# A fused attention and gated-MLP block: three head quads share the first layer norm's stage, two tiles are transposed by TensorE, and zero products stand first

## The chip, the cores and the metric

The kernel runs on one NeuronCore of a Trainium2 chip, as one program launched once. The metric is the device time of that launch in microseconds. TensorE (PE, with its weight loads PEld), VectorE (DVE), ScalarE (ACT), GpSimd (POOL) and SyncE (SP, used here only to issue DMAs) each run their own instruction stream in order and wait for each other by semaphores.

## What is computed

One transformer block in bf16 on a sequence of 2048 rows of 1024, with 32 query heads of 32 columns that share one key head and one value head, followed by a gated MLP of width 3584:

```python
q = (x @ wq).reshape(B, S, H, Dh).transpose(0, 2, 1, 3)   # x: layernorm of A_x
k = x @ wk
v = x @ wv
scores = einsum("bhqd,bkd->bhqk", q, k) * (Dh ** -0.5)
o = einsum("bhqk,bkd->bhqd", softmax(scores), v)
h = A_x + o.transpose(0, 2, 1, 3).reshape(B, S, H * Dh) @ wo
g, u = layernorm(h) @ w_gate, layernorm(h) @ w_up
out = h + (sigmoid(g) * u) @ w_down
```

The layer norms have no learned scale. The attention is not causal.

## The kernel before

**Tiles.** The 2048 rows are 16 tiles of 128 rows (`t`) or 8 chunks of 256 (`c`, `QC`). The 32 heads are 8 *quads* of four heads (`q`): 128 columns, each head in its own 32 partitions. Keys and values are cut in 8 blocks of 256 rows (`BPG`). A *burst* is the scores of one quad, one chunk and one key block: 8 matmuls that use 32 rows of the array each (`s_burst`, L525), which fill two of the three pairs of PSUM banks in `S_ps`. ACT turns each pair into P with one exponential over 128 x 1024 elements (`one_exp`, L549): two exponentials to a burst, 512 bursts, 1024 exponentials in all. A *PV group* (L640, L643) multiplies the P of one quad and chunk with V and, for the first ten groups, with ones for the row sums; later groups get their sums from DVE additions. Everything else on PE (K, Q, V, Wo, gate, up and down) goes through two further banks, `X_ps`, one open group to a bank.

**Where P lies.** P goes into a ring of 18 half tiles, `Pr`, so nine bursts deep. A burst may start only when PV has read the tile that it overwrites (`can_s`). P of quad 0 in chunk 0 lies in `hact` instead, six half tiles deep, since it is read along the way.

**First stage.** Each tile of x is loaded by SP. DVE takes its statistics (L314, L316); POOL computes 1/sqrt(var + eps) by two powers (L325, L327) for two tiles at once. The mean is subtracted on ACT for tiles 0 to 3 (L352) and on DVE for the others (L356); DVE multiplies (L359); SP issues a DMA transpose (L419) into `xnT`. Then K of two tiles (`k_group`), Q of chunk 0 (two quads first, the others along the way) and V (`vq_group`) can be computed. K, V and Q are evicted from PSUM by ACT (L434, L465, L470). Wk is copied to four places side by side by four ACT instructions (L932), so that K comes out once for each of the four row groups.

**The loop of the first stage** has eight turns, one for each key block. A turn takes the statistics of two tiles, normalizes two others, computes one burst of quad 0, K for the next block, one burst of quad 1, V (and in the later turns one quad of Q), and a part of quad 0's PV group. 16 bursts are done when it ends.

**The rest** is a fixed order, worked out at build time by a planner that keeps a clock for each engine: it issues a burst as soon as the exponentials before it have freed the banks, and fills PE's time in between with PV groups, the remaining Q groups, Wo groups, then gate, up and down of the chunks that are ready. Wo and w_down are loaded by POOL's queue; POOL also computes the second layer norm's roots. Gate and up weights are loaded by SP, in halves of 512 KB, also into parts of QT, Pr and kT that are free by then.

Of the kernel before, what the change touches and what calls it, by code (L numbers as in the profile page):

```python
# [12 lines left out]
P = 128  # L13
DH = 32
# [69 lines left out]
def bass_sequential_preLN__grouped_kv_mqa__glu_gated_glu__prompt_kernel(  # L84
# [32 lines left out]
    G_SUM, NPB = 10, 4  # L117
    WD_AT, WD_GAP, WD_LATE = 6, 6, 6
# [5 lines left out]
    with ExitStack() as es:  # L124
# [94 lines left out]
        def _(unused):  # L219
# [98 lines left out]
            def ln_rstd(i0, n, after):  # L318
                i1 = i0 + n
                need(pool, after)  # L320
                t_ = c_pool.inc(pool.tensor_scalar(out=vz[:, i0:i1], in0=mv[:, i0:i1, 1], scalar1=EPS_B, scalar2=None,  # L321
                                                   op0=ALU.add), 0.25)
                pool.tensor_copy(out=mean[:, i0:i1], in_=mv[:, i0:i1, 0])
                need(pool, t_)
                t_ = c_pool.inc(pool.tensor_tensor(out=sd[:, i0:i1], in0=vz[:, i0:i1], in1=half[:, 0:n], op=ALU.pow), 0.9)  # L325
                need(pool, t_)
                return c_pool.inc(pool.tensor_tensor(out=rs[:, i0:i1], in0=sd[:, i0:i1], in1=none[:, 0:n], op=ALU.pow), 0.8)  # L327
# [10 lines left out]
            NSUB = 4  # L338

            def ln1_stats(t):  # L340
                st_val[t] = ln_stats(x_tile(t), t, x_val[t])
                if t < NSUB:
                    need(pool, st_val[t])
                    nm_val[t] = c_pool.inc(pool.tensor_scalar(out=nmean[:, t:t + 1], in0=mv[:, t:t + 1, 0], scalar1=-1.0,
                                                              scalar2=None, op0=ALU.mult), 0.25)
                if t % 2 == 1:
                    rs_val[t - 1] = rs_val[t] = ln_rstd(t - 1, 2, st_val[t])

            def ln1_norm(t):
                if t < NSUB:  # L350
                    need(act, nm_val[t], xnT_read.get(t - 4))
                    xc = c_act.inc(act.activation(out=xn(t), in_=x_tile(t), func=ACTF.Identity, bias=nmean[:, t:t + 1]),  # L352
                                   0.91, 0.12)
                else:
                    need(dve, rs_val[t], xnT_read.get(t - 4))
                    xc = c_dve.inc(dve.tensor_scalar(out=xn(t), in0=x_tile(t), scalar1=mean[:, t:t + 1],  # L356
                                                     scalar2=None, op0=ALU.subtract), 0.5)
                need(dve, xc, rs_val[t])
                xn_val[t] = c_dve.inc(dve.tensor_scalar(out=xn(t), in0=xn(t),  # L359
                                                        scalar1=rs[:, t:t + 1], scalar2=None, op0=ALU.mult), 0.5)  # L360
                xnT_read[t] = xnT_val[t] = transposed(sp, xnT[:, t // TPQ, :, (t % TPQ) * P:(t % TPQ + 1) * P], xn(t), t % 4, xn_val[t])
                if t == 1:
                    for i in (8, 9):
                        load_x(i)
                if t == 3:
                    for i in (10, 11):
                        load_x(i)
                    load_wq(1, 256, 256)
                if t == 5:
                    for i in (12, 13):  # L370
                        load_x(i)
                if t == 7:
                    for i in (14, 15):
                        load_x(i)
                if t in (9, 11):
                    i = (t - 5) // 2
                    load_wq(i, 256 * i, 256)
# [51 lines left out]
            def k_group(p):  # L429
                c0 = 2 * p * P  # L430

                def evac(bank, tick):
                    need(act, tick)
# [4 lines left out]
                return _Group(items, evac, [wk4_val, xnT_val[2 * p], xnT_val[2 * p + 1]])  # L438
# [11 lines left out]
            def vq_group(p, qs):  # L450

                items, after = [], [xnT_val[0], xnT_val[1]] + [wq_need(q) for q in qs]
                for i, q in enumerate(qs):
                    items += q_items(q, 0, QC, i * QC)
                if p is not None:
                    after += [wv_val, xnT_val[2 * p], xnT_val[2 * p + 1]]
# [5 lines left out]
                def evac(bank, tick):  # L462
                    need(act, tick)
                    if p is not None:
                        v = v_val[p] = c_act.inc(act.activation(  # L465
                            out=V[:, 2 * p:2 * p + 2, :], in_=bank[:, QC:QC + 2 * DH].rearrange("p (a b) -> p a b", a=2),
                            func=ACTF.Copy), 0.2, 0.1)
                    if qs:
                        n = len(qs)
                        v = c_act.inc(act.activation(  # L470
                            out=QT[:, qs[0]:qs[0] + n, 0:QC], in_=bank[:, 0:n * QC].rearrange("p (a b) -> p a b", a=n),
                            func=ACTF.Copy), 0.1 + 0.22 * n, 0.1)
                        for q in qs:
                            q_val[(0, q)] = v
# [3 lines left out]
            def q_group(q, c0, n):  # L478
                def evac(bank, tick):
                    need(dve, tick)  # L480
# [613 lines left out]
```

## Time and profile before

| | us |
|---|---|
| median of 3 runs | 1138.39 |
| lowest and highest | 1138.31, 1139.34 |
| the profiled execution, whole | 1137.37 |
| its span in the trace | 1135.6 |
| PE busy / ACT busy / DVE busy | 1085.1 / 1012.3 / 803.1 |

One execution was profiled. A row of the timeline has the start and the length in us, the engine, the line of the kernel, the operation, the tile written and the tile read, their shapes and how many instructions the row joins; in brackets stands how long the engine was idle before it and what ended that. A row of the chain of waits has only start, length, engine, tile and line. A row of stretches has the stretch, its length, and for each engine its busy time and its instructions, then the clock granted to PE (1.00 is full speed), the mean share of the DMA engines and GB/s. PE's matmuls are pipelined and their ends are modelled, so PE that is busy is not PE at its peak.

### The profile page before, as it was taken

How to read it: one execution, taken by the hardware profiler on the slowest of the kernel's cores; microseconds unless marked ns; L12 is line 12 of the kernel's file. 1: busy time of each engine (PE TensorE's matmuls, PEld its weight loads, DVE VectorE, ACT ScalarE, POOL GpSimd, SP SyncE). 2: the span in 40 equal slices, each digit the busy share in tenths (PEclk: the TensorE clock that was granted, in tenths of full speed). 3: DMA queues.
4: the chain of work that ended last, by engine and by line, in shares of the span. 5: the costliest groups of instructions: out<-in, count | busy, mean ns of one | idle time of the engine just before them, and what ended most of it. 6: DMA issues, size and time to landing. Idle time of an engine off the chain costs nothing.

```text
span 1135.6 us, 33182 instructions
## 1 busy us (share of the span) xinstructions
PE 1085.1 (96%) x14450; PEld 655.8 (58%) x14512; DVE 803.1 (71%) x1424; ACT 1012.3 (89%) x1168; POOL 58.3 (5%) x122
## 2 busy tenths in 40 slices
PE   3899999999899999999999999999999999999998
PEld 2564446764376645774477645774376645775784
DVE  7433336878978798888987789788887898884111
ACT  4899999999999999999999999999999999991110
POOL 3210001000100000000100000000100010001000
PEclk9899999999999999999999999999999999999999
DMA  9931106871256613773166613663166612769700
GB/s 230 246 125 39 39 12 176 238 214 55 39 167 192 182 29 92 199 205 86 33 182 192 181 30 102 192 194 94 34 180 189 187 39 66 205 193 249 191 1 19
DMA packets 284176, 150.90 MB, mean 133 GB/s; under 512 B 40704, under 2 KB 278272, under 8 KB 284032
## 3 DMA queue, kind: packets, MB, share of 16 engines
q1 hardware_dynamic: 276256, 138.17, 45.1%
q0 software_dynamic: 2544, 9.44, 2.5%
q10 hardware_dynamic: 5232, 1.18, 0.8%
q8 instruction: 114, 1.87, 0.7%
q14 instruction: 30, 0.25, 0.1%
HBM read 136.18 MB, written 4.19 MB: 124 GB/s over the span
## 4 chain that ended last, share of the span: by engine, by line
PE 75%; ACT 12%; DVE 8%; issue 3%; DMA 1%; POOL 1%; ACTq 0%; DVEq 0%; another core or an unknown queue 0%
PE X_ps L792 33%; PE X_ps L856 13%; PE S_ps L525 11%; ACT Pr L549 11%; PE X_ps L304 8%; PE X_ps L643 8%; DVE pairs L582 2%; DVE pairs L591 2%; PE X_ps L640 1%; DVE st L314 1%; PE X_ps L622 1%; ACT hact L549 1%; DVE hx L866 0%; DMA zone<-hn 0%; DVE st L738 0%
## 5 line engine op out<-in xcount | busy, mean ns | idle before, releaser
L549 ACT ACTIVATE Pr<-S_ps 128x1024 bf16<-128x1024 f32 x1008 | 944.7, 1127 | 1.5 <-PE S_ps L525 1.4
L582 DVE TENSOR_TENSOR pairs<-Pr 128x1024 bf16<-128x1024 bf16 x432 | 293.1, 686 | 76.1 <-ACT Pr L549 73.1
L792 PE MATMUL X_ps<-QT,wgu 128*128 128x256 bf16 x2096 | 268.7, 274 | 3.3 <-DVE hx L866 1.6
L591 DVE TENSOR_TENSOR pairs<-pairs 128x1024 bf16<-128x1024 bf16 x324 | 223.8, 691 | 21.9 <-DVE pairs L582 0.5
L792 PEld LDWEIGHTS X_ps<-QT,wgu 128*128 128x128 bf16 x2096 | 192.2, 98 | 61.9 <-issue 39.3
L856 PE MATMUL X_ps<-zone,hact 128*128 128x512 bf16 x848 | 205.4, 380 | 8.1 <-issue 4.6
L525 PE MATMUL S_ps<-QT,kT 32*128 32x256 bf16 x4096 | 204.4, 274 | 7.7 <-ACT Pr L549 4.4
L792 PE MATMUL X_ps<-QT 128*128 128x256 bf16 x1328 | 168.5, 273 | 0.0
L643 PE MATMUL X_ps<-Pr,V 128*32 128x256 bf16 x4032 | 151.2, 274 | 2.0 <-DVE hact L831 1.2
L525 PEld LDWEIGHTS S_ps<-QT,kT 32*128 32x128 bf16 x4096 | 60.8, 92 | 153.1 <-ACT Pr L549 117.0
L792 PEld LDWEIGHTS X_ps<-QT 128*128 128x128 bf16 x1328 | 123.4, 98 | 30.8 <-issue 16.9
L811 ACT ACTIVATE gu<-X_ps 128x512 f32<-128x512 f32 x112 | 73.4, 656 | 76.0 <-PE X_ps L792 75.1
L856 PEld LDWEIGHTS X_ps<-zone,hact 128*128 128x128 bf16 x896 | 78.6, 98 | 106.9 <-issue 25.5
L831 DVE SCALAR_TENSOR_TENSOR hact<-gu,X_ps 128x512 bf16<-128x512 f32 x112 | 76.6, 684 | 66.3 <-PE X_ps L792 65.0
L643 PEld LDWEIGHTS X_ps<-Pr,V 128*32 128x32 bf16 x4032 | 99.9, 96 | 24.1 <-issue 16.5
L304 PE MATMUL X_ps<-zone 128*128 128x256 bf16 (+2 forms) x512 | 79.8, 302 | 22.2 <-POOL sd L325 14.2
L661 DVE COPY ols<-X_ps 128x256 f32<-128x256 f32 x64 | 26.9, 420 | 65.3 <-PE X_ps L643 55.1
L304 PEld LDWEIGHTS X_ps<-zone 128*128 128x128 bf16 x512 | 39.5, 101 | 53.6 <-POOL sd L325 14.2
L304 PE MATMUL X_ps<-wo,QT 128*128 128x512 bf16 x242 | 59.6, 380 | 1.7 <-issue 1.6
L866 DVE SCALAR_TENSOR_TENSOR hx<-X_ps,hx 128x512 bf16<-128x512 f32 x32 | 22.0, 688 | 41.7 <-PE X_ps L856 40.8
L321 POOL TENSOR_SCALAR vz<-mv 128x1 bf16<-128x1 bf16 (+1 forms) x24 | 8.8, 365 | 828.1 <-DVE mv L742 816.4
L481 DVE CAST QT<-X_ps 128x512 bf16<-128x512 f32 (+1 forms) x32 | 20.0, 624 | 33.2 <-PE X_ps L304 33.2
(53 smaller groups left out, 430.4 us busy)
## 6 DMA issues: line engine op xcount, KB each, us to landing
wgu<-in_B_w_gate_dram SPq DMA_DIRECT2D x73, 512.0 KB, 4.7
wgu<-in_B_w_up_dram SPq DMA_DIRECT2D x58, 512.0 KB, 4.6
QT<-in_B_w_up_dram SPq DMA_DIRECT2D x49, 512.0 KB, 4.9
QT<-in_B_w_gate_dram SPq DMA_DIRECT2D x34, 512.0 KB, 4.9
zone<-in_B_w_down_dram POOLq DMA_DIRECT2D x14, 512.0 KB, 5.1
hx<-in_A_x_dram SPq DMA_DIRECT2D x16, 256.0 KB, 3.5
out_dram<-hx SPq DMA_DIRECT2D x32, 128.0 KB, 1.7
Pr<-in_B_w_up_dram SPq DMA_DIRECT2D x5, 512.0 KB, 8.3
```

Source lines behind the costliest of these rows:

```text
L304: ins = pe.matmul(sel(bank), lhsT=a, rhs=b, start=(i == 0), stop=(i == last))
L525: ins = pe.matmul(S_ps[:, bank, kt * QC:(kt + 1) * QC], lhsT=kT4[DH * j:DH * (j + 1), (2 * b + kt) * P:(2 * b + kt + 1) * P], rhs=QT[DH * ...
L549: c_e.inc(act.activation(out=p_tile(k, n % 2).rearrange("p (a b) -> p a b", a=2), in_=S_ps[:, 2 * pr:2 * pr + 2, :], func=ACTF.Exp, scale= ...
L582: add_half[k] = slot_use[slot] = c_dve.inc(dve.tensor_tensor(out=pairs[:, slot, :].rearrange("p (j q) -> p j q", j=4), in0=p4[:, :, 0, :], ...
L591: slot_use[x] = slot_use[y] = c_dve.inc(dve.tensor_tensor(out=pairs[:, x, :], in0=pairs[:, x, :], in1=pairs[:, y, :], op=ALU.add), T_ADD, ...
L643: ins = pe.matmul(bank[DH * j:DH * (j + 1), 0:QC], lhsT=V[:, 2 * b + kt, :], rhs=rhs(j), start=first and summed, stop=last and not summed, ...
L661: dve.tensor_copy(out=ols[:, 0:QC], in_=bank[:, 0:QC])
L792: ins = pe.matmul(bank[:, j * QC:(j + 1) * QC], lhsT=halves[i][:, dt, j * P:(j + 1) * P], rhs=QT[:, dt, c * QC:(c + 1) * QC], start=(dt == ...
L811: tanh_val[n] = c_act.inc(act.activation(out=slot, in_=bank, func=ACTF.Tanh, scale=0.5), T_TANH, 0.1)
L831: hact_val[(c, 2 * fp + 1)] = gu_read[n] = c_dve.inc(dve.scalar_tensor_tensor(out=hact[:, 2 * fp:2 * fp + 2, :], in0=slot.rearrange("p (a ...
L856: ins = pe.matmul(bank, lhsT=hact[:, ft, tt * P:(tt + 1) * P], rhs=wd[:, ft, dc * 512:(dc + 1) * 512], start=(ft == 0), stop=(ft == NFT - 1))
L866: v = c_dve.inc(dve.scalar_tensor_tensor(out=hv, in0=bank, scalar=0.5, in1=hv, op0=ALU.mult, op1=ALU.add), 0.61, 0.08)
```

## The change

- **Loads.** The second quarter of Wq is loaded by SP between x tiles 3 and 4 (before: after tile 11). The other x tiles and quarters follow the transposes in an order given by a table, `LOADS`.
- **Zeros.** 36 matmuls of 128 x 256 zeros stand first in PE's order, and write to `X_ps`.
- **Tiles 0 and 1** are transposed by PE: 8 matmuls each against an identity matrix into the banks of `S_ps`, evicted to `xnT` by ACT (tile 0 and half of tile 1) and DVE (the other half). The identity is built by POOL.
- **Layer norm 1** computes the root for each tile by itself. ACT subtracts the mean for tiles 0 to 2 (before: 0 to 3).
- **Wk** is copied to four places by one DVE instruction.
- **Evictions** of V and of Q from quad 1 on go to DVE; K and quad 0's Q stay on ACT.
- **Three quads.** A turn of the loop has three bursts, one of each of quads 0, 1 and 2; 24 bursts are done when it ends. P of quad 2 lies in `wo` for the first four bursts and in the second half of the columns of `QT` for the other four. Wo's load, the w_down loads behind it, and the Q groups that write those columns wait until PV has read it.
- **The ring** keeps its depth, with an offset of two half tiles (`ring_need`, `p_tile`). The exponentials and PV address P as four columns of 256 rather than two of 512.

```diff
-            for t in range(8):
+            for t in range(4):
                 load_x(t)
...
+            load_wq(1, 256, 256)
+            for t in range(4, 8):
+                load_x(t)
+            warm = pairs[:, 1, 0:256]
+            ident = pairs[:, 0, 0:P]
+            warm_val = c_dve.inc(dve.memset(warm, 0.0), 0.2)
+            c_ = c_pool.inc(pool.memset(pairs[:, 2, 0:P], 1.0), 0.4)
+            need(pool, c_)
+            ident_val = c_pool.inc(pool.affine_select(out=ident, in_=pairs[:, 2, 0:P], compare_op=ALU.is_equal, fill=0.0,
+                                                      base=0, pattern=[[-1, P]], channel_multiplier=1), 0.5)
...
+            def pe_transpose(t):
+                need(pe, xn_val[t], ident_val)
+                for dt in range(DT):
+                    ins = pe.matmul(S_ps[:, 2 * t + dt // 4, dt % 4 * P:(dt % 4 + 1) * P], lhsT=xn(t)[:, dt * P:(dt + 1) * P],
+                                    rhs=ident, start=True, stop=True)
...
+            def pe_out(eng, t, h0, h1, *ticks):
+                need(eng, *ticks)
+                dst = xnT_tile(t)[:, 4 * h0:4 * h1, :]
+                src = S_ps[:, 2 * t + h0:2 * t + h1, :].rearrange("p a (b q) -> p (a b) q", q=P)
...
                 def evac(bank, tick):
-                    need(act, tick)
-                    if p is not None:
-                        v = v_val[p] = c_act.inc(act.activation(
...
+                    if qs == [0]:
+                        need(act, tick)
+                        v = c_act.inc(act.activation(out=out, in_=src, func=ACTF.Copy), 0.33, 0.1)
+                    else:
+                        need(dve, tick)
+                        if p is not None:
+                            v = v_val[p] = c_dve.inc(dve.tensor_copy(
...
             def burst(k):
-                if k < 2 * BPG:
-                    return 0, k % 2, k // 2
+                if k < HG * BPG:
+                    return 0, k % HG, k // HG
...
+            def ring_need(k):
+                r = ring(k)
+                if r is None or r < 2 * BPG + 1:
+                    return 0
+                return r - 2 * BPG if r <= 2 * BPG + BPG else r - BPG
...
             def p_tile(k, h):
                 r = ring(k)
                 if r is None:
...
-                return Pr[:, (2 * r + h) % RP, :]
+                elif r < BPG:
+                    t = Pr[:, 2 * r + h, :]
+                elif r < BPG + 4:
+                    i = 2 * (r - BPG) + h
+                    t = wo[:, i, :]
+                elif r < 2 * BPG:
+                    c0 = (r - BPG) * QC
+                    return QT[:, 4 * h:4 * h + 4, c0:c0 + QC]
+                else:
+                    t = Pr[:, (2 * r + 2 + h) % RP, :]
+                return t.rearrange("p (a b) -> p a b", b=QC)
...
+            need(pe, warm_val)
+            for i in range(NWARM):
+                pe.matmul(X_ps[:, 1, 0:256], lhsT=warm[:, 0:P], rhs=warm, start=True, stop=True)
+            k_pe[0] = 7.0
+            ln1_stats(0)
+            ln1_stats(1)
+            need(dve, wk_val)
+            wk4_val = c_dve.inc(dve.tensor_copy(out=wk4.rearrange("p a (r j) -> p a r j", r=4),
+                                                in_=wkr.unsqueeze(2).to_broadcast([P, DT, 4, DH])), 0.6)
+            ln1_sub(0)
+            ln1_sub(1)
+            ln1_mult(0)
+            f0, f1 = pe_transpose(0)
+            xnT_val[0] = [pe_out(act, 0, 0, 2, f0, f1)]
+            ln1_stats(2, (0,))
+            ln1_mult(1)
+            f0, f1 = pe_transpose(1)
+            ln1_stats(2, (1,))
+            xnT_val[1] = [pe_out(act, 1, 0, 1, f0), pe_out(dve, 1, 1, 2, f1)]
+            ln1_sub(2)
+            ln1_stats(3)
+            ln1_mult(2)
+            ln1_out(2)
+            ln1_sub(3)
             need(pe, const_val)
             run_group(k_group(0))
-            run_group(vq_group(None, [0, 1]))
+            run_group(vq_group(None, [0]))
+            run_group(vq_group(None, [1]))
+            ln1_mult(3)
+            ln1_out(3)
+            ln1_stats(4)
             pv[0] = pv_group(0)
             for p in range(BPG):
+                k0 = HG * p
+                s_burst(k0)
+                exps(k0)
+                if p == 0:
+                    run_group(vq_group(None, [2]))
+                    ln1_stats(5)
+                else:
+                    run_group(vq_group(p, [p] if p >= HG else []))
+                s_burst(k0 + 1)
+                exps(k0 + 1)
+                if p == 0:
+                    run_group(vq_group(0, []))
+                for t in (2 * p + 4, 2 * p + 5):
+                    if t < NT:
+                        ln1_norm(t)
                 for t in (2 * p + 6, 2 * p + 7):
                     if t < NT:
                         ln1_stats(t)
...
                 if p > 0:
                     run_item(pv[0])
                     run_item(pv[0])
+                s_burst(k0 + 2)
+                if p + 1 < BPG:
+                    exps(k0 + 2, (0,))
+                    run_group(k_group(p + 1))
+                    exps(k0 + 2, (1,))
+                else:
+                    exps(k0 + 2)
...
+                if wo_val[0] is None and pv_done[0] >= 2 * BPG:
+                    need(pool, (c_pv, 2 * BPG))
+                    wo_val[0] = dma(pool, wo[:], A_wo.rearrange("(q p) n -> p q n", p=P), d_wo, 2048)
```

More of the change, by code (lines that the diff above doesn't have):

```diff
@@ L369, in ln1_norm @@
[L369 to L377, printed above, removed]
+                    xc_val[t] = c_act.inc(act.activation(out=xn(t), in_=x_tile(t), func=ACTF.Identity, bias=nmean[:, t:t + 1]),
+                                          0.91, 0.2)
+                else:
+                    need(dve, mean_val[t], xnT_read.get(t - 4))
+                    xc_val[t] = c_dve.inc(dve.tensor_scalar(out=xn(t), in0=x_tile(t), scalar1=mean[:, t:t + 1],
+                                                            scalar2=None, op0=ALU.subtract), 0.45)
@@ L427, in _, with xnT_ready, k_group @@
             k_val, v_val, q_val = {}, {}, {}
-            def k_group(p):
+            def xnT_ready(*tiles):
+                r = []
+                for t in tiles:
+                    r += xnT_val[t] if isinstance(xnT_val[t], list) else [xnT_val[t]]
+                return r
+            def k_group(p, mid=None):
                 c0 = 2 * p * P
                 def evac(bank, tick):
+                    if mid is not None:
+                        mid()
                     need(act, tick)
@@ L888, in _ @@
             pv_next = [0]
[L889 removed]
+            wd_val, wo_val = [None], [None]
             pr_given = [False]
```

181 lines of the change are left out of this document (93 added, 88 removed).

## Prediction

> **What bounds the kernel now.** I read the page first, then four stretches of the span, then the timeline of the first 60 us and the chain of waits.
>
> ```profile
> span 1135.6 us, 33182 instructions
> PE 75%; ACT 12%; DVE 8%; issue 3%; DMA 1%; POOL 1%; ACTq 0%; DVEq 0%; another core or an unknown queue 0%
> ```
>
> ```profile
> 0.00:60.00 60.00, 34.59 (x484) 22.05 (x488) 34.29 (x76) 41.91 (x62) 18.85 (x44) 0.89 1.02 244
> 60.00:140.00 80.00, 79.78 (x1359) 42.54 (x1360) 27.06 (x59) 80.00 (x90) 5.67 (x8) 1.00 0.18 57
> 140.00:1025.00 885.00, 863.26 (x11879) 519.45 (x11936) 717.48 (x1250) 881.39 (x1004) 30.91 (x62) 1.00 0.49 135
> 1025.00:1136.00 111.00, 107.48 (x746) 71.77 (x740) 24.24 (x40) 8.96 (x15) 2.87 (x8) 1.00 0.47 111
> ```
>
> The columns are PE, PEld, DVE, ACT, POOL, then the granted clock and DMA. The chain names PE, but the stretches say more. From 60 to 1025 us ACT is busy for 961 of 965 us: the exponentials run without a gap, and PE fills the time between score bursts, with 21.7 us idle in the third row. From 1025 on only PE works, on what is left. So an exponential that ends earlier pulls the whole middle forward, as far as PE can follow, and PE work left over at its end is paid in full. The first 60 us are loose: PE is idle for 25 us, ACT for 18. That is the stage changed.
>
> ```profile
> 3.78 1.29 DVE L314 BATCH_NORM_STATS2 st<-hx 128x6 f32<-128x512 bf16 x2 [3.78 <-DMA hx<-in_A_x_dram]
> 5.40 0.25 POOL L344 TENSOR_SCALAR nmean<-mv 128x1 f32<-128x1 bf16 x1 [4.49 <-DVE mv L316]
> 9.02 0.88 DVE L359 TENSOR_SCALAR zone<-zone,rs 128x1024 bf16<-128x1024 bf16 x2 [2.32 <-POOL rs L327]
> 9.54 2.72 SPq L419 DMA_TRANSPOSE zone<-zone  x2
> 14.19 4.59 PE L304 MATMUL X_ps<-zone 128*128 128x256 bf16 x24 [14.19 <-POOL sd L325]
> 18.81 0.60 ACT L470 ACTIVATE QT<-X_ps 128x512 bf16<-128x512 f32 x1 [2.34 <-PE X_ps L304]
> 19.55 0.40 PE L525 MATMUL S_ps<-QT,kT 32*128 32x256 bf16 x8 [0.78 <-ACT QT L470]
> 19.98 1.94 ACT L549 ACTIVATE hact<-S_ps 128x1024 bf16<-128x1024 f32 x2 [0.57 <-PE S_ps L525]
> 26.63 1.87 PE L304 MATMUL X_ps<-zone 128*128 128x256 bf16 x8 [3.06 <-DMA zone<-zone]
> ```
>
> The first exponential starts at 19.98: two tiles wait for the slower reciprocal root (9.02), then for transposes by DMA (9.54 to 14.19, where the releaser shown, POOL, is long done), then 24 matmuls take 4.59 us. Later K groups wait for transposes again (26.63).
>
> **A, the start.** Tile 0 no longer waits for tile 1's statistics, and neither tile goes through a DMA. Three rows on POOL from the second layer norm give the chain for one column:
>
> ```profile
> 163.46 0.23 POOL L321 TENSOR_SCALAR vz<-mv 128x1 bf16<-128x1 bf16 x1 [30.59 <-DVE mv L742]
> 164.44 0.56 POOL L327 TENSOR_TENSOR rs<-sd,powers 128x1 f32<-128x1 bf16 x1
> 1059.71 48.91 PE X_ps L792 x448
> 1039.48 10.74 PE X_ps L856 x49
> ```
>
> From 163.46 to 165.00 is 1.54 us. The last two rows, of the chain, give PE's pace: 0.109 us for 256 columns, 0.219 for 512. Tile 0: mean at 5.65, root at 7.2, multiply (half of 0.88) to 7.75. Eight matmuls of 128 columns: no row; half the 256-column pace gives 0.44 us, the half-speed row at 26.63 (0.23 each) bounds it at 1.87; I take 0.44 and 0.2 for the result to arrive. Tile 1's chain queues behind tile 0's on POOL: mean 7.4, root 8.95, multiply to 9.5, transposes to 10.2, eviction (18.81: 0.60 for 512) to 10.9. The copy of Wk to four places moves to DVE between the two; bounded by one pass of 0.44 and the 1.3 us of ACT's four copies, it stands where DVE waits for tile 0's root, so 0 to 0.7 us; I take 0. K starts at 11.0, not 14.19. At full pace K, then the first Q quad take 0.87 each, Q's eviction ends at 13.4, a third group stands before the score burst, and the exponential follows 0.43 us after that (19.55 to 19.98 before): 14.5. Bounds: 13.7 if the third group hides, 16.5 if the 36 zero products leave the clock low and the 24 matmuls cost 4.59 again. The zeros end before 9 us at half pace (36 by 0.23), so they hide in PE's idle time; without that cover the two tiles would wait for them.
>
> **B, 24 bursts instead of 16.** ACT's pace in the loop:
>
> ```profile
> 43.11 1.94 ACT L549 ACTIVATE hact<-S_ps 128x1024 bf16<-128x1024 f32 x2 [0.18 <-PE S_ps L525]
> 44.93 0.39 ACT L434 ACTIVATE kT<-X_ps 128x256 bf16<-128x256 f32 x1
> 45.20 1.96 ACT L549 ACTIVATE Pr<-S_ps 128x1024 bf16<-128x1024 f32 x2
> 47.00 0.27 ACT L465 ACTIVATE V<-X_ps 128x64 bf16<-128x64 f32 x1
> 47.11 0.45 ACT L470 ACTIVATE QT<-X_ps 128x256 bf16<-128x256 f32 x1
> 47.81 1.94 ACT L549 ACTIVATE hact<-S_ps 128x1024 bf16<-128x1024 f32 x2 [0.26 <-PE S_ps L525]
> ```
>
> Starts differ by 1.82 us for two exponentials, 0.91 each, and 0.27 for kT. V and QT go to DVE and drop from ACT. Eight turns of 6 by 0.91 and 0.27, less the last kT: 45.6 us.
> ```profile
> 23.66 0.44 DVE L356 TENSOR_SCALAR hn<-wgu,mean 128x1024 bf16<-128x1024 bf16 x1
> 28.29 0.44 DVE L356 TENSOR_SCALAR zone<-wgu,mean 128x1024 bf16<-128x1024 bf16 x1
> ```
>
> DVE's turn, two tiles in 4.6 us, takes on V and QT (at ACT's 0.27 and 0.45): 5.3 against ACT's 5.7, still hidden, by 0.4 only. Behind DVE's wait for V stand the next two tiles, their transposes on SP, and so the K group one turn later.
>
> ```profile
> 26.93 5.18 DMA zone<-hn
> ```
>
> That is a transpose from issue to use. Tile 3 is multiplied by 14.9, so K for tiles 2 and 3 can start at 19.4 to 20.1 and its eviction at 20.5 to 21.2; ACT is there at 14.5 + 5 x 0.91 = 19.05. It loses 1.5 to 2.1 us. By the same count it loses 0.4 to 1 in the second turn. I take 3.9 in all, between 1.5 and 8 (up to 1 us in each of the eight turns). The 48th exponential ends at 14.5 + 45.6 + 3.9 = 64.0; from the bounds 61 to 70. Before, burst 24 can be read in the chain:
>
> ```profile
> 64.98 0.11 PE X_ps L640 x4
> 65.09 0.11 PE X_ps L643 x4
> 75.35 0.33 PE S_ps L525 x8
> ```
>
> It starts when the 47th exponential has ended, so the 48th ends near 76.2. Gain at this point: 12.2 us.
>
> **C, what is given back.** In the order of the built program 18 half bursts of PV, at 0.22 us each by the two rows at 65 us, stand between bursts 32 and 33: P of the second and third quads must be read before the ring takes burst 33. That is 4.0 us of PV and 0.4 of Q, against 1.8 us of exponentials in hand: ACT waits 2.6. From burst 64 to 512 the new order holds 32 more matmuls of 512 columns and 18 fewer of 256: 5.0 us, with 11 more changes of kind (0.1 each) 6.1 us of PE work. PE was idle for 21.7 us there, so most of it fits; I take 1.5, between 0 and 6.1. After the last burst 18 more matmuls of 256 stand: 2.0 us, paid in full. The exponentials' new views, four columns of 256, cover the same 1024 elements; I take 0, and a loss would show in each of 1024. Wo waits on POOL for the third quad's PV, with w_down's loads and the second layer norm behind it; that is near 85 us, and the first use was long after, so nothing:
>
> ```profile
> 156.79 1.03 PE L304 MATMUL X_ps<-wo,QT 128*128 128x512 bf16 x4
> ```
>
> On SP one wq load passes x tiles 4 to 7, which DVE reaches at 15: nothing.
>
> Sum: -12.2 + 2.6 + 1.5 + 2.0 = **-6.1 us**. The profiled execution took 1137.37 us (1135.6 of span); that gives 1131.3. The median is 1.0 above it, so **1132.3**.
>
> **Rivals.** *PE is the bound.* PE's stretches are over 97% busy, and the chain gives PE 75%. Then none of the 6.1 us fits into idle time: -12.2 + 2.6 + 6.1 + 2.0 = -1.5, **1136.9**. Against it: ACT alone is without gaps, and PE's order waits at bursts for exponentials.
>
> *The clock drops in the loop* (slower).
>
> ```profile
> 23.17 0.40 PE L525 MATMUL S_ps<-QT,kT 32*128 32x256 bf16 x8 [0.85 <-ACT Pr L549]
> 21.00:24.00 3.00, 1.71 (x37) 0.90 (x34) 2.93 (x7) 3.00 (x7) 0.63 (x2) 1.00 1.12 320
> 24.00:27.00 3.00, 0.37 (x2) 0.28 (x3) 2.89 (x8) 1.98 (x4) 2.01 (x4) 0.62 1.14 229
> 33.00:36.00 3.00, 2.98 (x21) 1.60 (x19) 2.93 (x7) 1.80 (x4) 2.18 (x4) 0.50 1.20 175
> 36.00:39.00 3.00, 3.00 (x49) 1.85 (x48) 2.86 (x8) 1.60 (x4) 1.27 (x3) 0.60 1.01 236
> 32.21 1.86 PE X_ps L304 x8
> 34.64 2.29 PE X_ps L304 x24
> 37.91 0.60 PE S_ps L525 x8
> ```
>
> The granted clock falls to half near 24.7, after a thin stretch, and is back near 38.4. PE's early turns are thinner still: three bursts, V and K are about 2.9 us of work in 5.7. At half pace a turn with a Q group costs K 1.86, Q and V 2.29, PV 0.98 (from 36.93 to 37.91), three bursts of 0.6 and five switches, 7.4 against 5.73: 1.7 lost in each of five turns; in the two before, the path from burst through K to kT (2.7 against 1.82) loses 0.85 each. Together 10.1 us: -6.1 + 10.1 = +4.0, **1142.4**. It decides from 6 us lost on, four such turns. For it: the drop is in the trace. Against: the Q turns are dense, and dense work brought the clock back.
>
> [...]
>
> *The start does not get faster*: the one-column chains and evictions cost what the DMA did, first exponential at 18.5. Then -2.1, **1136.3**. Nothing in the rows speaks for it but the unmeasured operations.
>
> **How the numbers follow.** My forecast 0.62; PE-bound 0.20; clock 0.14; start 0.04. A measurement here tells about 0.2%, 2.3 us, from no change. The forecast's own range is 1127 (48th exponential at 60.5, no friction: -11.1) to 1135.5; the second and fourth cases lie within 2.3 us of before, the third above. So faster 0.62, same 0.24, slower 0.14. The range goes from 1127 to 1141, which leaves out the clock's worst and little below.
>
> **What would show it.** First exponential near 14.5; ACT's gap before the second kT 1.5 to 2 us; 48th exponential near 64; an ACT gap near 2.6 us before burst 33; last exponential about 8 us earlier; the PE-only end 2 us longer. Wrong if the granted clock reads 0.5 between 20 and 60 us, if ACT shows waits for PE after 100 us that sum to over 4 us, or if K groups wait for transposes in most turns.

## The result, and the profile after

The median went from 1138.35 us (4 runs, 1137.22 to 1139.34) to **1132.09 us** (4 runs, 1131.51 to 1133.32): a ratio of 0.9947, 95% interval 0.993 to 0.9964. That is 6.3 us less; the forecast was 1132.3. The profiled execution of the changed kernel is the longest of its four, 1133.32 us with 1131.6 of span, and that of before lies 1.0 us under its median, so the two traces differ by only 4.0 us of span. Both numbers are needed below.

First the page's head and chain, then the same four stretches as before (the boundary moved from 1025 to 1015 us, since the exponentials end earlier):

```profile
span 1131.6 us, 33334 instructions
PE 66%; DVE 10%; issue 2%; ACT 2%; POOL 1%; DVEq 0%; another core or an unknown queue 0%; ACTq 0%
```

```profile
0.00:60.00 60.00, 42.85 (x540) 26.28 (x540) 39.42 (x93) 45.26 (x54) 27.01 (x73) 0.80 0.81 183
60.00:140.00 80.00, 78.29 (x1361) 42.95 (x1353) 26.88 (x60) 77.19 (x86) 5.39 (x7) 1.00 0.26 84
140.00:1015.00 875.00, 859.64 (x11775) 515.90 (x11833) 711.61 (x1244) 872.46 (x994) 35.38 (x64) 1.00 0.49 136
1015.00:1132.00 117.00, 113.20 (x834) 75.66 (x838) 28.28 (x47) 12.67 (x20) 3.00 (x8) 1.00 0.48 118
```

The middle looks as before. The first 60 us are fuller on PE and on ACT, but the granted clock (third number from the end) fell from 0.89 to 0.80, and from 60 to 140 us ACT is now idle for 2.8 us.

The start on PE, then ACT's first exponentials and waits for K in the loop, from the changed kernel's timeline:

```profile
1.11 5.69 PE L1011 MATMUL X_ps<-pairs 128*128 128x256 bf16 x36 [1.11 <-DVE pairs L259]
8.09 0.62 PE L414 MATMUL S_ps<-pairs,zone 128*128 128x128 bf16 x8 [1.29 <-DVE zone L389]
10.04 0.62 PE L414 MATMUL S_ps<-pairs,zone 128*128 128x128 bf16 x8 [1.33 <-DVE zone L389]
11.54 4.27 PE L316 MATMUL X_ps<-zone 128*128 128x256 bf16 x24 [0.88 <-POOL vz L339]
```

```profile
16.18 1.94 ACT L632 ACTIVATE hact<-S_ps 128x1024 bf16<-128x1024 f32 x2 [0.82 <-PE S_ps L609]
22.65 0.38 ACT L495 ACTIVATE kT<-X_ps 128x256 bf16<-128x256 f32 x1 [1.78 <-PE X_ps L316]
36.62 0.39 ACT L495 ACTIVATE kT<-X_ps 128x256 bf16<-128x256 f32 x1 [1.90 <-PE X_ps L316]
...
68.09 16.71 ACT L632 ACTIVATE Pr<-S_ps 128x1024 bf16<-128x1024 f32 x18
87.61 12.94 ACT L632 ACTIVATE Pr<-S_ps 128x1024 bf16<-128x1024 f32 x14 [2.81 <-PE S_ps L609]
```

K starts at 11.54, close to the 11.0 of the prediction; the transposes cost 0.62 us for eight, the two tiles' multiplications end 0.3 and 0.5 us later than expected. But the 24 matmuls take 4.27 us instead of 2.6. The row at 68.09 begins with the 49th exponential, the first one behind the loop. In the trace of before that one begins at 75.7 (a row of four starts with the 48th at 74.80, and the pitch is 0.91). The windows of 3 us show why the 24 matmuls are slow:

```profile
6.00:9.00 3.00, 1.42 (x16) 0.92 (x13) 2.07 (x5) 2.07 (x3) 2.54 (x6) 1.00 1.19 305
9.00:12.00 3.00, 1.08 (x11) 0.81 (x12) 2.47 (x6) 2.26 (x3) 1.31 (x4) 0.87 1.14 331
12.00:15.00 3.00, 3.00 (x18) 2.13 (x17) 1.77 (x4) 0.74 (x3) 2.55 (x6) 0.56 0.31 93
...
24.00:27.00 3.00, 2.17 (x45) 0.95 (x41) 2.65 (x7) 3.00 (x4) 2.68 (x8) 0.50 1.00 240
27.00:30.00 3.00, 2.44 (x36) 1.37 (x29) 2.36 (x5) 2.69 (x4) 0.88 (x3) 0.79 0.70 118
...
36.00:39.00 3.00, 2.43 (x18) 1.20 (x17) 0.49 (x2) 2.38 (x4) 2.24 (x6) 0.50 1.17 269
```

PE works 2.5 us of the six between 6 and 12, with no gap over 1.33 us; then the clock is at half while most of the 24 matmuls run, and again in most of the windows from 21 to 42 us. A clock of 0.87 and then 0.56 in windows of 3 us, with half speed as the lower level, is 0.78 + 2.64 = 3.4 us at half, so it fell at 11.22. In the 3.41 us ahead of that, as long as the stretch at half, PE was busy for 1.24:

```profile
7.81:11.22 3.41, 1.24 (x16) 0.90 (x16) 2.51 (x6) 2.67 (x4) 1.63 (x4) 1.00 1.21 295
```

So the clock fell here behind a stretch in which PE was thinly used, and not idle for longer than 1.33 us at a time.

### The profile page after: what moved, and what is told of

Read it like the earlier page. It is cut to its first block, busy times and chain, and to the rows that moved or that the text cites. A ratio compares the mean times of both kernels' runs of the same rounds, so it can differ in the third digit from the quotient of the medians.

```text
span 1131.6 us, 33334 instructions
## 1 busy us (share of the span) xinstructions
PE 1094.0 (97%) x14498; PEld 660.8 (58%) x14564; DVE 806.2 (71%) x1443; ACT 1007.6 (89%) x1151; POOL 70.8 (6%) x152
## 4 chain that ended last, share of the span: by engine, by line
PE 66%; DVE 10%; issue 2%; ACT 2%; POOL 1%; DVEq 0%; another core or an unknown queue 0%; ACTq 0%
PE X_ps L875 35%; PE X_ps L939 11%; PE S_ps L609 10%; PE X_ps L726 7%; DVE pairs L666 3%; DVE pairs L675 3%; PE X_ps L316 2%; ACT Pr L632 2%; DVE st L821 1%; PE X_ps L706 1%; DVE hx L803 1%; DVE hn L348 0%; DVE hx L949 0%; POOL sd L342 0%; DVE ols L752 0%
## 5 line engine op out<-in xcount | busy, mean ns | idle before, releaser
L632 ACT ACTIVATE Pr<-S_ps 128x1024 bf16<-128x1024 f32 x992 | 932.2, 1127 | 6.7 <-PE S_ps L609 6.6
L875 PE MATMUL X_ps<-QT,wgu 128*128 128x256 bf16 x2096 | 265.6, 273 | 0.2 <-issue 0.2
L875 PEld LDWEIGHTS X_ps<-QT,wgu 128*128 128x128 bf16 x2096 | 192.2, 98 | 55.1 <-issue 31.7
L726 PE MATMUL X_ps<-Pr,V 128*32 128x256 bf16 x3968 | 148.4, 274 | 1.1 <-ACT gu L894 0.9
L894 ACT ACTIVATE gu<-X_ps 128x512 f32<-128x512 f32 x112 | 74.7, 667 | 76.0 <-PE X_ps L875 75.7
L331 POOL CAST mean<-mv 128x1 f32<-128x1 bf16 x29 | 8.5, 292 | 802.2 <-DVE mv L825 784.9
```

Of the source, the lines that this page charges most:

```text
L632: c_e.inc(act.activation(out=p_tile(k, n % 2), in_=S_ps[:, 2 * pr:2 * pr + 2, :].rearrange("p a (b q) -> p (a b) q", q=QC), func=ACTF.Exp, ...
L726: ins = pe.matmul(bank[DH * j:DH * (j + 1), 0:QC], lhsT=V[:, 2 * b + kt, :], rhs=rhs(j), start=first and summed, stop=last and not summed, ...
L875: ins = pe.matmul(bank[:, j * QC:(j + 1) * QC], lhsT=halves[i][:, dt, j * P:(j + 1) * P], rhs=QT[:, dt, c * QC:(c + 1) * QC], start=(dt == ...
L894: tanh_val[n] = c_act.inc(act.activation(out=slot, in_=bank, func=ACTF.Tanh, scale=0.5), T_TANH, 0.1)
```

## The experiments

Every version is the changed kernel with the edit shown; e5 holds e4's edit too, and e8 those of e5 and e6. e10 and e11 leave a part of the computation out. "49th" is where the 49th exponential begins (with three quads, the first one behind the loop), "last" where the 1024th ends, all in the profiled execution. The ratio is to the kernel before, run on the same chip in the same batch. (The versions of one batch share their runs of before, whose median was 1138.48, 1138.67 and 1140.02 us in the three batches; so ratios, not medians, are compared between batches.)

| version | first exp. | 49th | last | span | median | ratio, 95% |
|---|---|---|---|---|---|---|
| before | 19.98 | 75.7 | 1024.3 | 1135.6 | 1138.35 | 1 |
| changed | 16.18 | 68.09 | 1018.8 | 1131.6 | 1132.09 | 0.9947 (0.993-0.9964) |
| e1_no_zeros | 16.73 | 67.49 | 1018.3 | 1131.0 | 1132.05 | 0.9944 (0.9924-0.9964) |
| e2_two_quads | 14.69 | 76.09 | 1027.7 | 1138.7 | 1141.64 | 1.0036 (1.0022-1.005) |
| e3_dma_tiles | 20.64 | 72.04 | 1023.4 | 1136.1 | 1136.93 | 0.9985 (0.9973-0.9998) |
| e4_hold_start | 14.74 | 67.27 | 1016.5 | 1129.2 | 1131.04 | 0.9936 (0.9919-0.9954) |
| e5_hold_loop | 14.81 | 64.97 | 1014.2 | 1126.9 | 1129.43 | 0.9917 (0.9895-0.9939) |
| e6_wq_early | 14.74 | 66.65 | 1017.8 | 1130.5 | 1131.57 | 0.9934 (0.9914-0.9954) |
| e7_more_pe | 16.35 | 68.64 | 1025.2 | 1138.8 | 1138.46 | 0.9994 (0.9979-1.0008) |
| e8_all | 14.78 | 65.07 | 1015.9 | 1128.6 | 1130.51 | 0.9928 (0.9908-0.9949) |
| e9_down_pe | 16.34 | 67.49 | 1020.0 | 1133.6 | 1135.54 | 0.9964 (0.9952-0.9976) |
| e10_less_pe | 16.13 | 67.51 | 1017.5 | 1129.4 | 1131.35 | 0.9932 (0.9917-0.9946) |
| e11_less_down | 14.67 | 66.81 | 1017.0 | 1128.9 | 1130.56 | 0.993 (0.9915-0.9944) |

The table reads almost as one rule. In every version with three quads and the middle left alone, the last exponential ends 949.2 to 951.3 us after the 49th begins, and the span ends 112.7 to 112.8 us after that. Whatever brings the 49th exponential forward reaches the end.

### Which part carries the gain

**Two quads** in the loop, with the new start; the third quad's eight bursts follow the loop:

```diff
-    HG = 3
+    HG = 2
...
-                    run_group(vq_group(None, [2]))
```

> The changed kernel with two quads in a turn instead of three; start, zeros, evictions and the homes of P stay. Theory (a turn is set by layer norm and transposes at about 5.6 us, and the third quad fills what ACT would idle): the first exponential stays at 16.2, the 32nd ends near 61, the 48th near 76, as before the change; the wait of 2.8 us before burst 33 goes; time 1136 to 1138. Rival (the gain is the earlier start, 3.8 us at the first exponential, and the third quad brings little): time 1133 to 1134.5.

The 49th exponential begins at 76.09, as late as before, although the first began 5.3 us earlier. ACT waited for K in every turn, and the third quad's bursts stood behind the loop:

```profile
20.44 0.38 ACT L495 ACTIVATE kT<-X_ps 128x256 bf16<-128x256 f32 x1 [2.89 <-PE X_ps L316]
26.92 0.38 ACT L495 ACTIVATE kT<-X_ps 128x256 bf16<-128x256 f32 x1 [2.43 <-PE X_ps L316]
34.93 0.38 ACT L495 ACTIVATE kT<-X_ps 128x256 bf16<-128x256 f32 x1 [3.02 <-PE X_ps L316]
```

An early start alone is thus swallowed by this loop, whose turn is set by the tiles and by K; the third quad fills ACT's time in it. (K's group stands behind both bursts of a turn here, and stood between them before the change, so it is not quite the loop of before.) Where the time then came out is a miss: 1136 to 1138 was expected, and 1141.64 was measured. The 49th exponential came as expected, but from there to the end of the last it took 951.6 us, against 948.6 before the change, and the waits for PE that are listed for ACT on this way are 4.5 us against 1.9. Why this order waits more is open.

**Tiles 0 and 1 by DMA** again:

```diff
-            f0, f1 = pe_transpose(0)
-            xnT_val[0] = [pe_out(act, 0, 0, 2, f0, f1)]
+            ln1_out(0)
```

and the same for tile 1.

> The changed kernel with tiles 0 and 1 transposed by DMA again. Their multiplies end at 8.0 and 10.0; a transpose lands about 5 us after its issue, so K starts at 15 instead of 11.5 and the first exponential comes at 19.7 instead of 16.2. Theory (what ACT loses at the start is carried to the end, less the 1.8 us that it waits for the second K group anyhow): time 1133.8 to 1135.6. Rival (the start is hidden by the loop's own waits for transposes): time 1132.1 to 1132.9.

The start came 4.46 us later, the 49th exponential 3.95 and the span 4.5. The loop gives only 0.5 us of a late start back, so the transposes by PE are worth nearly all of it. That is more than the 1133.8 to 1135.6 expected: the first exponential came at 20.64 and not at 19.7, and while the wait before the second kT went, as expected, the one before the fourth grew from 1.90 to 3.26.

### The clock

> The changed kernel without its 36 zero products; all else as in the changed kernel. In the changed kernel they end at 6.8 us, the granted clock falls to half at 11.2 and is back at 14.6, so the 24 matmuls of K and Q take 4.27 us all the same. Theory (the zeros warm too early and bring nothing): first exponential at 16.2 to 16.8 instead of 16.18, time 1132.1 to 1132.7. Rival (they do hold the clock for the transposes and for K): the transposes and K cost 1.5 us or more in addition, first exponential at 17.7 or later, time 1133.6 or more.

```diff
-    NWARM = 36
+    NWARM = 0
```

The time is the same. The zeros end at 6.80 and the clock is low again while K runs, so as placed they bring nothing in the median (1132.05 us without them, 1132.09 with them). Then the gaps of the start were filled too, with 46 zeros first and 10 and 8 more behind the transposes of tiles 0 and 1:

```diff
-    NWARM = 36
+    NWARM = 46
...
+            hold(10)
...
+            hold(8)
```

> The changed kernel with 46 zero products first, ten more after tile 0's transposes and eight after tile 1's, so that PE has no long gap before K. Theory (the clock falls at 11.2 for lack of work before it): the clock stays at 1.00 until the loop, K and Q's 24 matmuls take 2.8 us instead of 4.3, first exponential at 14.7, time 1130.6 to 1131.6. Rival (products with zeros, or so few of them, do not hold the clock): first exponential at 16.2 or later, time 1132.1 or more.

The first exponential moved to 14.74, 0.24 us from the prediction's 14.5. That alone does not show that the zeros hold the clock, for e2, e6 and e11 begin at 14.67 to 14.74 without the added ones (told under e6). The windows say more: from 6 to 12 us PE works 5.76 of the six us in e4, and the clock reads 1.00 up to 18; in e9, with 36 zeros alone, it works 2.72, and the clock reads 0.94 from 9 to 12 and 0.50 from 12 to 15. All three versions with the added zeros (e4, e5, e8) read 1.00 up to 18 and take 2.78 us for the 24 matmuls. In e4 the clock fell near 18.8 us instead (0.63 from 18 to 21, then 0.50), and K's waits in the loop grew (the longest to 2.79), so the 49th gained only 0.8. With zeros at the head of the first V and K groups of the loop as well:

```diff
-                    run_group(vq_group(p, [p] if p >= HG else []))
+                    held_group(vq_group(p, [p] if p >= HG else []), 5 if p < HG else 0)
...
-                    run_group(vq_group(0, []))
+                    held_group(vq_group(0, []), 5)
...
-                    run_group(k_group(p + 1))
+                    held_group(k_group(p + 1), 8 if p < 4 else 0)
```

> The kernel with the clock held at the start, and zero products in the loop too: five at the head of V's group in the first three turns, eight at the head of K's group in the first four. There the clock was at half from 20 to 43 us, and ACT waited 6.2 us for PE in the loop. Theory (half a clock makes K late and so ACT idle): clock near 1.00 through the loop, ACT's waits in the loop about 4 us, 48th exponential ended near 65.3 instead of 67.3, time near 1129. Rival (the waits are those for the transposes, whatever the clock): clock up, 48th exponential still at 67, time 1130.7 to 1131.3.

```profile
9.00:12.00 3.00, 3.00 (x35) 2.42 (x32) 2.34 (x5) 2.38 (x4) 1.31 (x4) 1.00 1.14 332
12.00:15.00 3.00, 3.00 (x34) 2.34 (x32) 2.31 (x6) 1.41 (x4) 2.59 (x6) 1.00 0.29 89
...
24.00:27.00 3.00, 1.87 (x20) 1.23 (x21) 2.05 (x8) 2.10 (x3) 2.23 (x6) 0.95 0.62 206
27.00:30.00 3.00, 2.44 (x18) 1.19 (x17) 2.83 (x7) 1.73 (x3) 1.27 (x4) 0.50 0.94 193
30.00:33.00 3.00, 2.32 (x54) 1.51 (x53) 2.08 (x6) 3.00 (x4) 1.89 (x5) 0.98 1.00 227
36.00:39.00 3.00, 2.11 (x54) 1.38 (x51) 1.93 (x6) 3.00 (x4) 1.82 (x5) 1.00 1.16 326
```

The clock is at half in one window only: of the twelve windows of 3 us from 9 to 45 us one reads under 0.9, against nine in the changed kernel. ACT's waits for K in the loop are 0.73, 2.17, 0.51 and 0.51, in all 3.92 us, and the 49th exponential begins at 64.97, 3.1 us earlier than in the changed kernel; e8, with the same zeros, begins it at 65.07, and the eight versions with three quads and PE's transposes but without zeros in the loop at 66.65 to 68.64. The median is 1129.43, the fastest of all versions (its ratio's interval and the changed kernel's just overlap). Work that computes nothing shortens the kernel here, and the clock is higher where the path from transposes to K needs it.

**Wq's last two quarters loaded first**, right behind x tile 7 instead of along the way, in the changed kernel (e6) and in e5 (e8):

```diff
+            load_wq(2, 512, 256)
+            load_wq(3, 768, 256)
...
-            LOADS = {2: (8,), 3: (9,), 5: (10, 11), 6: ("q2",), 7: (12,), 8: ("q3",), 9: (13, 14), 11: (15,)}
+            LOADS = {2: (8,), 3: (9,), 5: (10, 11), 7: (12,), 9: (13, 14), 11: (15,)}
```

> The changed kernel with the third and fourth quarter of Wq loaded right behind x tile 7 instead of between the transposes of tiles 6 to 9. Theory (the 512 KB between tile 6's and tile 7's transposes makes the fourth K group late, where ACT waits 1.90 us): that wait falls below 1 us, time 1131.0 to 1131.6. Rival (the 1 MB now collides with the transposes of tiles 2 and 3): the wait before the second kT grows from 1.78 us by as much, time 1132.1 or more.

> The clock held at the start and in the loop, and Wq's quarters loaded early. Theory (both causes of ACT's waits in the loop are real and add): 48th exponential ended near 64.5, time near 1128. Rival (only the start counts): time 1130.5 to 1131.3, as with the start alone.

No gain: 0.5 us in the median of e6, inside the runs' spread, and with e5's zeros the time is not under e5's, so e8's expectation of 1128 fell. The traces show two effects that nearly cancel. What was hoped for came: the wait before the fourth kT fell from 1.90 us to 0.69 in e6. But the rival's sign came with it. The second K group waits for the transpose of tile 3, here in e5, then in e8, which differ in Wq's loads alone, with the clock at 1.00 for both groups:

```profile
19.15 1.03 PE L316 MATMUL X_ps<-zone 128*128 128x256 bf16 x8
```

```profile
20.61 1.03 PE L318 MATMUL X_ps<-zone 128*128 128x256 bf16 x8 [1.54 <-DMA zone<-hn]
```

The wait before that kT is 0.73 us in e5 and 2.21 in e8. One pair of executions does not prove the collision: in e11, without the early loads, this group begins as late, at 20.42. e6 also shows the clock take another course over the same work. Up to the first exponential its work on PE is the changed kernel's, and yet:

```profile
1.11 6.94 PE L1013 MATMUL X_ps<-pairs 128*128 128x256 bf16 x36 [1.11 <-DVE pairs L261]
11.59 2.78 PE L318 MATMUL X_ps<-zone 128*128 128x256 bf16 x24 [0.88 <-POOL vz L341]
14.74 1.94 ACT L634 ACTIVATE hact<-S_ps 128x1024 bf16<-128x1024 f32 x2 [0.82 <-PE S_ps L611]
20.96 1.86 PE L318 MATMUL X_ps<-zone 128*128 128x256 bf16 x8 [2.92 <-DMA zone<-hn]
22.86 0.38 ACT L497 ACTIVATE kT<-X_ps 128x256 bf16<-128x256 f32 x1 [3.44 <-PE X_ps L318]
```

The zeros were slower (6.94 us against 5.69): the window from 3 to 6 us has 16 of them, and 23 in the changed kernel, so they ended at 8.05 instead of 6.80. The clock fell later too, near 20.6, and the 24 matmuls ran at full pace in 2.78 us. From 6 to 12 us PE worked 3.69 of the six us instead of 2.50, and the clock stayed behind them:

```profile
6.00:9.00 3.00, 2.66 (x22) 1.88 (x20) 2.13 (x5) 2.07 (x3) 2.51 (x7) 1.00 1.18 305
9.00:12.00 3.00, 1.03 (x12) 0.85 (x13) 2.41 (x6) 2.26 (x3) 1.31 (x4) 1.00 1.13 332
12.00:15.00 3.00, 3.00 (x34) 2.33 (x33) 2.25 (x6) 1.42 (x4) 2.59 (x6) 1.00 1.17 315
```

Of this gain nothing is left at the second kT, whose wait is 3.44 us against 1.78. That is mostly not the clock: ACT is there 1.44 us earlier, but the K group begins at 20.96, as in the changed kernel (21.08), since the transpose of tile 3 came no sooner; only 0.3 us more are from slower matmuls (1.86 us against 1.54). e11 shows the same pair (2.78 and 2.97). The seven executions with this start and 36 zeros fall into two groups. In e2, e6 and e11 the window from 3 to 6 us has 16 zeros, PE works 3.20 to 3.69 of the six us from 6 to 12, and the clock reads 1.00 from 12 to 15; in the changed kernel, e7, e9 and e10 it has 21 or 23, PE works 2.41 to 2.72, and the clock reads 0.50 to 0.58. The same 36 zeros took 5.63 us in e10 and 6.94 in e6; why is not shown.

### The middle: which engine sets the pace

The prediction let all but 1.5 of 6.1 us of PE work vanish in PE's idle time. Four versions test it with 7.0 us each, of which 6.1 lie before the last exponential (64 products of 256 columns, or 32 of 512, at 0.109 and 0.219 us): more in the gate and up groups (e7), more in the down groups (e9), less in the gate and up groups (e10), less in the down groups (e11).

```diff
+                            if dt == 0 and fp < 2:
+                                pe.matmul(bank[:, j * QC:(j + 1) * QC], lhsT=halves[i][:, 0, j * P:(j + 1) * P],
+                                          rhs=QT[:, 0, c * QC:(c + 1) * QC], start=True, stop=True)
```

> The changed kernel with 64 matmuls of 256 columns more, each the first product of a gate or up group done twice, eight to a chunk; the order is the same otherwise. That is 7.0 us of PE work, 6.1 of it before the last burst and 0.9 behind it. Theory (ACT sets the pace up to the last exponential and PE has some 20 us of idle time there): 0.9 us at the end and at most 1.5 of the rest show, time 1133.0 to 1134.5. Rival (PE is the bound): all of it shows, time 1139.

```diff
+                        if ft == 0 and c < NQC - 1:
+                            for _ in range(2 if c < 4 and tt == dc == 0 else 1):
+                                pe.matmul(bank, lhsT=hact[:, 0, tt * P:(tt + 1) * P],
+                                          rhs=wd[:, 0, dc * 512:(dc + 1) * 512], start=True, stop=True)
```

> The changed kernel, with the first product of the down projection's groups of the first seven chunks done 32 times more (512 columns each, some 7.0 us of TensorE work, as much as the doubled gate and up products), order of everything else unchanged. Theory (the bound alternates: in the 64-us windows with the gate and up products TensorE was busy 63.8 of 64, in those with the down products 62 of 64, with 2 us over in each of seven): at most 2 us of the 7 are paid, 1132-1134. Rival (TensorE sets the pace everywhere): 1138.5, as with the gate and up products.

```diff
+                            ins = None
+                            if dt or fp > 1:
...
+                                                start=(dt == (0 if fp > 1 else 1)), stop=(dt == DT - 1))
```

> The changed kernel without the first of the products in the gate and up groups of the first two feature pairs of each chunk: 64 matmuls of 256 columns (7.0 us of TensorE work) fewer, a part of the computation left out, order unchanged. Theory (TensorE sets the pace in these stretches): 4 to 7 us shorter than the changed kernel, 1125-1128. Rival (ScalarE's exponentials set it everywhere, and added work alone shows): 1131.5-1132.1.

```diff
+                        ins, lo = None, 0 if c == NQC - 1 else 2 if c < 4 and tt == dc == 0 else 1
+                        if ft >= lo:
...
+                                            rhs=wd[:, ft, dc * 512:(dc + 1) * 512], start=(ft == lo), stop=(ft == NFT - 1))
```

> The changed kernel without 32 of the products of 512 columns in the down projection of the first seven chunks (7.0 us of TensorE work fewer, a part of the computation left out), order unchanged. Theory (in these stretches ScalarE sets the pace): 1131-1132.1, nothing gained. Rival (TensorE sets the pace everywhere): 1125.5.

From the 49th exponential's begin to the end of the last it took 950.7 us in the changed kernel, 956.5 in e7, 952.5 in e9, 950.0 in e10 and 950.2 in e11. So of the 6.1 us, 5.8 were paid in e7 and 1.8 in e9, and taking the work away brought 0.7 and 0.5; the 0.9 us behind the last exponential were paid, or saved, in full in all four (112.7 us in the changed kernel, 113.6 in e7 and e9, 111.9 in e10 and e11). e9's 1.8 may be too low as a price: its execution shows no fall of the clock in the middle, and the changed kernel's does (last section). Against the 949.2 us of e4 and e5, which show none either, it paid 3.3. Whether the added work itself kept the clock up was not tested. My expectation for e7 fell, and with it the view that PE has room everywhere; the one for e10 fell too, since less work in these stretches did not help. e9's median came 1.5 us above its range, in a batch whose runs of before were 1.7 us longer too, and e11's 0.4 below its own. Two neighbouring stretches, the first mostly gate and up, the second mostly down, of the changed kernel and then of e9, show the room:

```profile
332.00:396.00 64.00, 63.79 (x884) 42.83 (x887) 51.17 (x89) 64.00 (x76) 0.00 (x0) 1.00 0.65 184
396.00:460.00 64.00, 61.93 (x823) 32.54 (x823) 55.39 (x99) 63.83 (x72) 4.18 (x8) 1.00 0.31 84
```

```profile
332.00:396.00 64.00, 64.00 (x869) 42.57 (x869) 51.07 (x88) 63.57 (x75) 0.00 (x0) 1.00 0.65 184
396.00:460.00 64.00, 63.94 (x839) 32.73 (x839) 54.98 (x98) 63.88 (x72) 4.18 (x8) 1.00 0.30 83
```

In the first stretch both engines are full; in the second PE had 2 us over, and e9 filled them. ACT sets the pace of the middle and PE follows without a margin in the gate and up stretches. In e7 the loss hardly shows as waiting. ACT's list of waits behind 76 us (line, what it waited for, us in all, times, longest), for the changed kernel and for e7:

```profile
ACT Pr L632 <- PE S_ps L609: 5.0, 5, 2.8
```

```profile
ACT Pr L632 <- PE S_ps L609: 6.2, 10, 2.8
ACT gu L897 <- PE X_ps L878: 0.4, 2, 0.2
```

And the busy times of the whole span as one stretch, again of the changed kernel and of e7:

```profile
0.00:1140.00 1140.00, 1093.99 (x14498) 660.79 (x14564) 806.19 (x1443) 1007.59 (x1151) 70.78 (x152) 0.99 0.48 132
```

```profile
0.00:1140.00 1140.00, 1101.13 (x14562) 667.22 (x14628) 806.58 (x1443) 1010.70 (x1151) 70.64 (x152) 0.99 0.49 132
```

1.6 us more of waits are listed, while ACT's busy time grew by 3.1 us for the same instructions. Consecutive exponentials overlap (two take 1.94 us, but start 0.91 apart, so one takes 1.03). By these lengths an operand that is late by less than the overlap of 0.12 us lengthens the busy time and leaves no gap; that this is where the 3.1 us went is argued, not tested.

## Why the prediction was right, and where its steps were off

**The shape was right.** The third quad in the loop and the transposes by PE are both needed, the gain is made before 70 us, and a part is given back later. The predicted -6.1 us met -6.3 in the medians, more closely than the terms deserve. The traces of single executions say -4.0, and there the terms can be compared one by one:

- **A, the start**: 14.5 predicted, 16.18 measured, inside the bounds of 13.7 to 16.5. (No row of before stood behind the 0.2 us for a result to arrive; tile 0's eviction on ACT began at 8.84 and tile 1's half on DVE at 10.75, 0.13 and 0.09 us behind the end of the transposes.) The reason is the one named for the upper bound: the zeros left the clock low, and the 24 matmuls cost 4.27 us. With the clock held (e4, e5) the first exponential came at 14.74 and 14.81, so the count of steps was right and the clock was what it missed. What decides which of the two comes no run shows: of seven executions with this start, three began at 14.67 to 14.74 (e2, e6, e11) and four at 16.13 to 16.35. The sentence that the zeros "hide in PE's idle time" held (they begin at 1.11, which its count to 9 us left out, and end at 6.80); that they do nothing in the median (e1) it did not say.
- **B, the loop**: 3.9 us of waits predicted, 5.6 measured; the pace without them 45.6 predicted and 46.3 measured. With the clock held (e5) the waits were 3.92, but in other turns than counted (0.73 and 2.17 in the first two, 1.5 to 2.1 and 0.4 to 1 predicted), so that this sum agrees is luck. So is the second kT's wait of 1.78 in the changed kernel: ACT and the second kT both came about 1.8 us later than counted, and where ACT came as counted (e6, e11) the wait was 3.44 and 2.97. So the rival of the clock was partly true: the clock reads 0.50 in the loop, as the prediction's last paragraph named for a sign of being wrong, but it cost about 2 us and not 10. At the 49th exponential the gain was 75.7 - 68.1 = 7.6 instead of 12.2: this is the term that was mis-sized, 1.7 by A, some 2.4 by B, and 0.5 by reading the row of before as 76.2.
- **C, what is given back**: the wait before burst 33 was 2.81 (2.6 predicted). Of 7.6 us, 5.4 remained at the last exponential, so 2.2 were given back on the whole way instead of 4.1. The work behind the last exponential grew by 1.4 instead of 2.0. The count of PE's extra work used 0.1 us for a change of kind, and no row was given for it; the trace of before shows it, since 13 products of 256 columns and the change to the next burst span 1.52 us (200.43 to 201.95), 0.10 more than 13 by 0.109. PE's extra work in the middle cost next to nothing here. e9 bears that out only in part for matmuls of 512 columns in the down stretches, and e7 shows that in the gate and up stretches it would have been paid, so that PE has idle time there was not reason enough.

**The sum**: -7.6 + 2.2 + 1.4 = -4.0 in the traces. Two errors, a gain taken too large by 4.6 and a return taken too large by 2.5, cancelled in part. So it is in part luck that the median was met within 0.2 us. The remaining 2 us to the medians are the spread of single executions: the same start and loop (in e6 with other loads) gave a 49th exponential at 68.09 in the changed kernel and between 66.65 and 68.64 in e6, e7, e9, e10 and e11, and the profiled execution of before was 1 us quicker than its median.

**The rivals.** "The start does not get faster" fell with the first exponential at 16.18, and e3 shows what the transposes by DMA would have left. "PE is the bound" gave 1136.9 and fell for the time, though added work does show in the gate and up stretches (e7). What is open: how much of the given-back 2.2 us is the ring's wait alone, since the order was not tried without it.

## What to carry to other kernels

A stage at the start that feeds a saturated middle is worth its full length (with three quads and the middle left alone, the 1024th exponential ended 949.2 to 951.3 us after the 49th began, early or late), so compare versions by the moment at which the saturated engine's first work behind that stage begins. Before adding work to an engine that looks 2% idle, look at the stretches in which the work would lie: of the same 6.1 us, 5.8 were paid in one kind of stretch and 1.8 to 3.3 in the next, and taking them away brought less than 1 in either. Where a stage is thin on TensorE, look at the granted clock in windows of a few us, and fill the gaps up to the work that matters: that brought the ratio from 0.9947 to 0.9917 here (e5), and zeros that end before the gap did nothing (0.9944 without them, e1).

## What the hardware showed that was not expected

The clock's fall without a long gap, and its two courses over the same start, are told above. In the changed kernel's trace PE was busy for 0.88 to 2.00 of the 3.41 us ahead of each of five falls, at 11.2, 21.5, 31.7, 55.6 and 683.6 us, so it was idle through none of them. What decides a fall these figures do not tell: in e6 PE was busy for 1.03 of the 3.00 us from 9 to 12, and the clock read 1.00 up to 18. The fall happens in the middle too. In the changed kernel's down stretch PE is busy for half of four microseconds, and the clock is then low for 0.32 + 3.04 = 3.4 us (worked out as above, with half as the lower level):

```profile
680.00:684.00 4.00, 2.03 (x23) 0.66 (x21) 3.86 (x8) 4.00 (x5) 0.00 (x0) 0.96 0.02 4
684.00:688.00 4.00, 4.00 (x19) 1.14 (x17) 3.79 (x8) 2.79 (x4) 0.00 (x0) 0.62 0.10 35
```

ACT waits 1.21 us there. The executions of e4 and e5 show no such fall behind 76 us, and from the 49th exponential to the last they took 949.2 us, against 950.7 to 951.3 in the changed kernel, e1, e3, e6 and e8, which all show one there. e9 shows none either; e7, e10 and e11 show one. Second, the clock column reads 1.00 from 0 to 6 us although the 36 zeros take 0.156 to 0.193 us each, against 0.109 at full pace, so the column does not show the rise of their pace (in the changed kernel the us from 2 to 3 has 6 of them, the one from 5 to 6 has 12).
